# Passes of score products with up to four heads, and up to two blocks for VectorE in each

## The chip, the cores and the metric

The kernel runs on one core of a Trainium2 chip. The time is device time in microseconds of one execution; several runs give a median. TensorE (PE in the profile) does the matrix products, ScalarE (ACT) and VectorE (DVE) work on their results in PSUM, GpSimd (POOL) works on SBUF, and the queues of SyncE (SP) and ScalarE start the transfers.

## What is computed

Two attention layers read the same input of 2048 rows and 512 columns, and a gate mixes them. Layer A is softmax attention with 32 heads of 16 columns, layer B is linear attention.

```python
def _A_ref(x, wqkv, wo):
    ...
    q, k, v = qkv[0], qkv[1], qkv[2]
    scores = jnp.einsum("bhqd,bhkd->bhqk", q, k) * (Dh ** -0.5)
    p = _softmax(scores, axis=-1)
    o = jnp.einsum("bhqk,bhkd->bhqd", p, v)
    return (lambda x, *d: x.transpose(*d))(o, 0, 2, 1, 3).reshape(B, S, D) @ wo

def _B_ref(x, wqkv, wo):
    ...
    phi = lambda t: jnp.where(t > 0, t + 1, jnp.exp(t)) + 1e-6
    pq, pk = phi(q), phi(k)
    kv = jnp.einsum("bhsd,bhse->bhde", pk, v)
    z = jnp.einsum("bhsd->bhd", pk)
    num = jnp.einsum("bhqd,bhde->bhqe", pq, kv)
    den = jnp.einsum("bhqd,bhd->bhq", pq, z)[..., None] + 1e-6
    ...

g = _sigmoid((x * gate_w).sum(-1, keepdims=True))
return g * a + (1 - g) * b
```

## The kernel before

**Blocks and rounds.** A block is the score product of one head, 128 keys and 512 queries: a PSUM bank of 128 x 512. A round is four heads (every second one of a group of eight, each on its own 32 rows of the systolic array) and 512 queries. It has 16 blocks of keys for each of four heads, so 64 blocks; there are 32 rounds, 2048 blocks in all. Four products of four different heads lie on different rows of the array and can run together; the head of a block u is u % 4.

**Two ways to the exponential.** Most blocks go to ScalarE: an `ACTIVATE` with Exp (L2038) reads two or three banks at once and writes bf16 to the tile `PT` (20 slots of one block). The others are "claimed" for VectorE, which forms an approximate exponential in integers: L1558 writes 16-bit integers whose bits are read as a float16 (tile `DP`, 13 buffers of four blocks each). For four claimed blocks together two more versions are made, each shifted by a constant; these adds run on VectorE (L1599) or on POOL (L1602), whichever the planner thinks sooner. So a claimed block has three products with V, a ScalarE block one. Only the last 6 of 16 key blocks of a round can be claimed (`KB2 = 10`).

**PSUM.** Eight banks. The ring has two slots, `SLOTS = [(0, 3), (3, 3)]`: banks 0 to 2 and 3 to 5. ScalarE reads one slot while TensorE fills the other. The first two banks of a slot hold a pair; the third (bank 2 or 5, a "third" below) makes it a triple, or holds a claimed block. Bank 6 holds the sum of P V of the round. Bank 7 (`misc_banks`) serves the other work, and claimed blocks; banks 6 and 7 swap roles between rounds.

**The planner.** The program is laid down at build time by a planner written in Python, which keeps an estimate of each engine's time (`PE.t`, `AC.t`, `DV.t`, `PO.t`) and puts each instruction into the fixed order of its engine. The engines follow their order, with semaphores between them. Nothing is decided on the chip. One turn of the main loop (from L1969) makes one *pass*: the score products of two or three ScalarE blocks and perhaps a claimed one, then the exponential, and then, until the next slot is free, it fills TensorE's time with P V (`pv_step`), pieces of other work (`misc_step`) or idle products that keep TensorE's clock up (`fill`).

- P V runs in sets of four products, one for each head, on different columns of the array; `MOST` limits the sets that are laid down in a row. `PV_LAG`, `PT_URGENT` and `ROOM` steer when.
- The other work is a list of steps in chains, each with a due time in passes of three blocks: the projections Q, K and V of the next head groups and the gate (A chain), layer B (B chain), the output rows and partial sums (O chain), and some early steps. A step takes bank 7, runs in pieces of matmuls, and then queues an eviction, mostly on VectorE (`push(1, ...)`).
- VectorE's queue takes items by priority: 0 for what ends a round and for a block claimed within a pass, 1 for evictions of steps and blocks claimed otherwise, 3 for the adds. `dve_load` is the planner's estimate of the work waiting there.

Before the change a block is claimed in three ways: within a pass of a pair (`claim_in_group`, in a third, or in bank 7 when no step is due); right behind a triple (`claim_beside`, in bank 7); or between two passes with a score product by itself (`misc_step`, in bank 7, if `dve_load` is under `CLAIM_LOAD`). A pass of a triple is made when its third is free within `WAIT3` and no block can be claimed.

The core of the loop before:

```python
eb = next((b for b in (b0 + 2, 7 - (b0 + 2)) if is_free(b, soon)), None)
if eb is None and not reserved() and hold[0] is None and due_step(PE.t)[0] is None:
    eb = bank_free(PE.t + 0.02)
...
if len(us) == 2 and g > last_stage:
    extra = claim_in_group(PE.t, [j for j in range(4) if j not in [u % 4 for _, u in us]])
    if extra is not None or eb != b0 + 2:
        break
```

`L685` is the line of the helper through which nearly all matmuls are issued; the profile tells them apart by their tiles (`Qpad,KT` scores, `PT,Vaug` and `DP,Vaug` P V, `warm` idle products). L970 is the exponential of layer B's features on ScalarE.

Of the kernel before, what the change touches and what calls it, by code (L numbers as in the profile page):

```python
# [17 lines left out]
STATS = {}  # L18
# [35 lines left out]
NTRI = 4  # L54
HINT_AT = 150
KB2 = 10
# [129 lines left out]
LAT = 0.11  # L186
SET_T = 0.218
MM512 = 0.216
QK_T = 0.324
# [23 lines left out]
def bass_gated_mix__mha_block__linear_attn_block__prompt_kernel(  # L213
# [26 lines left out]
    LAST_ORDER = [(2, 0), (2, 1), (2, 2), (3, 0), (3, 1), (3, 2), (2, 3), (3, 3)]  # L240
    pairs_ = [(t8, qc) for t8 in range(NT8 - 2) for qc in range(NQC)] + LAST_ORDER
    KV0, KV1 = 1.0, 1.2
    PRE_T = 3
    PRE_GAP = 5
    OUT_GAP = 8

    with ExitStack() as es:
        _cnt = [0]
# [345 lines left out]
        def dve_load(now):  # L594
            return max(0.0, DV.t - now) + sum(o[3] * (ADD_W if len(o) > 6 else 1) for it in items for o in it.ops)
# [95 lines left out]
        def f_tr(o, i):  # L691
# [12 lines left out]
           dur=1.6)  # L704
# [67 lines left out]
        def is_free(b, now):  # L772
            return b not in bank_busy and not r_bank[b].pend and max(r_bank[b].tr + LAT, r_bank[b].tw + 0.05) <= now

        def bank_free(now):
            best = None
            for b in misc_banks:
                if b in bank_busy or r_bank[b].pend:
                    continue
                t = max(r_bank[b].tr + LAT, r_bank[b].tw + 0.05)  # L780
                if t <= now and (best is None or t < best[0]):
                    best = (t, b)
            return None if best is None else best[1]
# [394 lines left out]
        def unit_aps(r, u):  # L1178
            t8, qc, half = rounds[r]
            kb, j = u // 4, u % 4  # L1180
            kt = KT[32 * j:32 * j + 32, t8 % 2, 128 * kb:128 * (kb + 1)]
            q = Qpad[32 * j:32 * j + 32, r % NQS, :]
            return kt, q, [r_KT[t8 % 2][kb // 4], r_Q[r % NQS]]
# [3 lines left out]
        def skip(r):  # L1187
            while head[r] < NU and head[r] in taken[r]:
                head[r] += 1
# [4 lines left out]
        def next_unit():  # L1194
# [7 lines left out]
                act_round[0] += 1  # L1202
            return None

        acc_round = [0]
        acc_n = [0]
        fresh = [True]
# [115 lines left out]
        def v_ready(r, u):  # L1323
            return (rounds[r][0], u // 16) in v_done

        PT_URGENT = 11

        started = set()
        done_j = {}
# [280 lines left out]

        Q_OFF = -4
        GPR = 14.8
        B0 = 0.8
        B1 = 21
        chains = []

# [98 lines left out]
        def due_step(now):  # L1715
            load = dve_load(now)
            due = None
            for ch in chains:
                if not ch:
                    continue  # L1720
                st = ch[0]
                if (st.target > cur_g[0] and not hurry()) or not step_ready(st, now):
                    continue
                key = st.target - (A_FIRST if ch is a_chain else 3 * A_FIRST if ch is e_chain else 0)
                if due is None or key < due[2]:
                    due = (st, ch, key)
            return due, load

        def reserved():

            return acc_n[0] >= RES_FROM or (fresh[0] and acc_round[0] > 0 and r_bank[acc_bank[0]].pend)

        def behind_by():

            return max([cur_g[0] - ch[0].target for ch in chains if ch] or [0])

        def claim_beside(now, js):

            if hold[0] is not None or reserved():
                return  # L1740
            b = bank_free(now)
            if b is None:
                return
            due, load = due_step(now)
            if load >= CLAIM_LOAD or (due is not None and (load > STARVE or cur_g[0] > due[0].target + late())):
                return
            c = can_claim(now, js)
            if c is not None:
                claim(c[0], c[1], b, True)

        def claim_in_group(now, js):

            if hold[0] is None and not reserved() and due_step(now)[0] is None and bank_free(now + 0.3) is not None:
                return None
            if dve_load(now) >= (RING_LATE if behind_by() > BEHIND else RING_LOAD):
                return None
            return can_claim(now, js)

        def misc_step(now, t_late):

            if hold[0] is not None:
                if now + (SWITCH_T if pe_mode[0] == "full" else 0.0) + hold[0][2][0][2] > t_late + OVER:
                    return False
                if hold[0][2][0][3] < 0.05 and mac_until(now + 0.35) < GATE_MAC and (hold[0][0].spare or (not fresh[0] and not r_bank[acc_bank[0]].pend)):
                    return False
                cont_step()
                return True
            b = None if reserved() else bank_free(now)
            if b is None:
                if behind_by() <= THIRD or lent[0] is not None:  # L1770
                    return False
                due, load = due_step(now)
                if due is None or due[0].keeps or now + FIRST_T > t_late + OVER:
                    return False
                b3 = next((b for b in (2, 5) if is_free(b, now)), None)
                if b3 is None or not is_free(7 - b3, t_late + WAIT3):
                    return False
                STATS["thirds"] = STATS.get("thirds", 0) + 1
                due[1].popleft()
                start_step(due[0], b3)  # L1780
                return True
            due, load = due_step(now)
            c = can_claim(now, (0, 1, 2, 3)) if load < CLAIM_LOAD else None
            if due is not None and (c is None or load > STARVE or cur_g[0] > due[0].target + late() or hurry()):
                if now + FIRST_T > t_late + OVER:
                    return False
                due[1].popleft()
                start_step(due[0], b)
                return True
            if c is not None and load < LATE_CLAIM and now + QK_T < t_late:  # L1790
                claim(c[0], c[1], b, False)
                return True
            return False
# [18 lines left out]
            STATS["fills"] = STATS.get("fills", 0) + 1  # L1812
            return True

        WAIT3 = 0.2
        THIRD = 30
        HURRY = 40
        CLAIM_FREE = 2
        FORCE_N = 1
        MOST = 3  # L1820
        OVER = 0.15
        FIRST_T = 0.43
        ROOM = 0.4
        CLAIM_LOAD = 3.7
        LATE_CLAIM = 4
        STARVE = 6
        MAC_LOW = 0.45
        MAC_END = 0.45
        FILL_T = 0.2
        FILL_AHEAD = 0.9  # L1830
        END_FROM = 44
        RING_LOAD = 3.9
        RING_LATE = 4
        BEHIND = 30
        LEND = 900
        RES_FROM = 60
        MARGIN = 0.15
        PV_LAG = 13
        LATE = 8
        LAG_END = 12  # L1840
        A_FIRST = 200
        LATE_END = 0
# [1 line left out]
        def late():  # L1844
            return LATE_END if act_round[0] >= NR - 2 else -9 if e_chain else LATE

# [121 lines left out]
        last_stage = max(stage)  # L1968
        while True:  # L1969
            us = []  # L1970
            extra = None
            b0 = SLOTS[g % 2][0]
            if lent[0] is not None and is_free(lent[0], PE.t + 0.02):
                lent[0] = None
# [2 lines left out]
            if g > last_stage and lent[0] is None and hold[0] is None and (behind_by() > LEND or (e_chain and LEND_E)) and bank_free(PE.t + 0.3) is None:  # L1977
                due, _ = due_step(PE.t + 0.3)
                if due is not None and not due[0].keeps:
                    lend = due  # L1980
            eb = None
            if g > last_stage:
                soon = PE.t + WAIT3
                eb = next((b for b in (b0 + 2, 7 - (b0 + 2)) if is_free(b, soon)), None)
                if eb is None and not reserved() and hold[0] is None and due_step(PE.t)[0] is None:
                    eb = bank_free(PE.t + 0.02)
            while len(us) < SLOTS[g % 2][1]:
                if len(us) == 2 and (away or lend is not None):
                    break
                if len(us) == 2 and g > last_stage and eb is None:  # L1990
                    break
                if len(us) == 2 and g > last_stage:
                    extra = claim_in_group(PE.t, [j for j in range(4) if j not in [u % 4 for _, u in us]])
                    if extra is not None or eb != b0 + 2:
                        break
                u = next_unit()
                if u is None:
                    break
                us.append(u)
# [21 lines left out]
            for k, (r, u) in enumerate(us):  # L2021
                kt, q, rr = unit_aps(r, u)
                fns.append(f_mm(RINGB[b0 + k], kt, q))
                for res in rr:
                    if res not in rd:
                        rd.append(res)
            if extra is not None:
                kt, q, rr = unit_aps(*extra)
                fns.append(f_mm(bank_ap(eb), kt, q))
                rd += [res for res in rr if res not in rd]  # L2030
            pe_macro(fns, reads=rd, writes=[r_bank[b0 + k] for k in range(len(us))] + ([r_bank[eb]] if extra is not None else []), dur=QK_T, mac=0.053 * len(fns), mode="rows")
            if extra is not None:
                claim(extra[0], extra[1], eb, True, in_group=True)
                STATS["in_group"] = STATS.get("in_group", 0) + 1
            elif g > last_stage and len(us) == 3:
                claim_beside(PE.t, [j for j in range(4) if j not in [u % 4 for _, u in us]])
            n = 512 * len(us)
            op(AC, lambda p0=p0, b0=b0, n=n: nc.scalar.activation(  # L2038
                PT[:, 512 * p0:512 * p0 + n], ps[:, 512 * b0:512 * b0 + n], ACT.Exp, scale=LN2 / FRAC, bias=LN_KAPPA),
# [290 lines left out]
```

## Time and profile before

| | us |
|---|---|
| median of 3 runs | 685.74 (684.61 to 687.06) |
| the profiled execution | 684.7 |
| its span, from the first to the last instruction | 683.0 |
| ScalarE, two banks: 585 instructions, duration of one | 1.218 |
| ScalarE, three banks: 81 instructions, duration of one | 1.649 |
| VectorE, claimed block: 635 instructions, duration of one | 0.685 |

A row of the groups reads: line, engine, operation, output and input tiles, shapes, count, busy time of the group, mean nanoseconds of one, and then the idle time of the engine just before them with what ended it. Busy time counts overlapping instructions once, so count times mean can be more. In the timeline a row is: start, duration, engine, line, operation, tiles, shape, count, and in brackets the idle time before it. TensorE's granted clock is 1.000 over the whole span.

### The profile page before, as it was taken

How to read it: one execution, taken by the hardware profiler on the slowest of the kernel's cores; microseconds unless marked ns; L12 is line 12 of the kernel's file. 1: busy time of each engine (PE TensorE's matmuls, PEld its weight loads, DVE VectorE, ACT ScalarE, POOL GpSimd, SP SyncE). 2: the span in 40 equal slices, each digit the busy share in tenths (PEclk: the TensorE clock that was granted, in tenths of full speed). 3: DMA queues.
4: the chain of work that ended last, by engine and by line, in shares of the span. 5: the costliest groups of instructions: out<-in, count | busy, mean ns of one | idle time of the engine just before them, and what ended most of it. 6: DMA issues, size and time to landing. Idle time of an engine off the chain costs nothing.

```text
span 683.0 us, 18997 instructions
## 1 busy us (share of the span) xinstructions
PE 661.9 (97%) x8009; PEld 201.3 (29%) x8011; DVE 575.8 (84%) x961; ACT 666.8 (98%) x706; POOL 508.9 (75%) x289
## 2 busy tenths in 40 slices
PE   8999999999999999999999999999999999999997
PEld 4322222333223222222322323322332222222223
DVE  4488888889888988996789898997989998898584
ACT  5999999999999999999999999999899999999995
POOL 5097899686679797787468898776887687977770
PEclk9999999999999999999999999999999999999999
DMA  9800101000010001102001010100211201010111
GB/s 225 241 3 9 27 2 33 3 18 18 2 34 2 18 18 39 28 2 63 4 17 26 10 35 17 25 12 19 48 24 36 38 19 41 16 42 18 28 37 46
DMA packets 44815, 22.95 MB, mean 34 GB/s; under 512 B 33976, under 2 KB 40568, under 8 KB 44728
## 3 DMA queue, kind: packets, MB, share of 16 engines
q1 hardware_dynamic: 42712, 20.12, 12.9%
q10 hardware_dynamic: 2016, 1.57, 0.9%
q8 instruction: 66, 1.08, 0.6%
q14 instruction: 21, 0.17, 0.1%
HBM read 8.00 MB, written 2.10 MB: 15 GB/s over the span
## 4 chain that ended last, share of the span: by engine, by line
ACT 89%; PE 9%; DVE 1%; issue 0%; DMA 0%; SPq 0%; POOL 0%; DVEq 0%; ACTq 0%; POOLq 0%
ACT PT L2038 87%; PE ps L685 9%; ACT epool L970 2%; PE ps L692 0%; DMA rsum<-oraw 0%; DVE DP L2140 0%; DVE DP L1558 0%; DVE epool L1397 0%; DVE OT L1278 0%; DVE epool L1398 0%; DVE phi L975 0%; SPq L604 0%; DVE KT L859 0%; DVE rraw L1272 0%; DVE DP L2145 0%
## 5 line engine op out<-in xcount | busy, mean ns | idle before, releaser
L2038 ACT ACTIVATE PT<-ps 128x1024 bf16<-128x1024 f32 (+1 forms) x666 | 654.7, 1270 | 2.5 <-PE ps L685 2.3
L1602 POOL TENSOR_TENSOR DP<-DP,step 128x1024 int32<-128x1024 int32 x256 | 485.6, 1923 | 149.4 <-DVE DP L1599 50.2
L1558 DVE TENSOR_SCALAR DP<-ps 128x512 int16<-128x512 f32 x635 | 417.1, 685 | 59.3 <-PE ps L685 54.7
L685 PE MATMUL ps<-Qpad,KT 32*128 32x512 bf16 x2048 | 270.8, 384 | 13.4 <-ACT PT L2038 7.5
L685 PE MATMUL ps<-DP,Vaug 128*32 128x512 f16 x1890 | 191.0, 384 | 0.7 <-POOL DP L1602 0.2
L685 PE MATMUL ps<-PT,Vaug 128*32 128x512 bf16 x1402 | 153.5, 384 | 0.8 <-DVE Vaug L914 0.5
L685 PEld LDWEIGHTS ps<-Qpad,KT 32*128 32x128 bf16 x2048 | 67.3, 91 | 276.7 <-ACT PT L2038 250.5
L685 PEld LDWEIGHTS ps<-DP,Vaug 128*32 128x32 bf16 x1890 | 47.3, 95 | 67.0 <-issue 40.6
L685 PEld LDWEIGHTS ps<-PT,Vaug 128*32 128x32 bf16 x1402 | 36.4, 94 | 50.3 <-issue 41.3
L1599 DVE TENSOR_SCALAR DP<-DP 128x2048 int16<-128x2048 int16 (+1 forms) x62 | 45.9, 771 | 0.4 <-PE ps L685 0.4
L685 PE MATMUL ps<-warm 128*32 128x512 bf16 (+1 forms) x232 | 38.5, 390 | 1.1 <-POOL step L735 1.1
L685 PE MATMUL ps<-xT,wA 128*32 128x512 bf16 x432 | 32.3, 384 | 0.0
L1299 DVE COPY oraw<-ps 128x512 f32<-128x512 f32 x31 | 21.1, 681 | 3.3 <-PE ps L685 3.1
L970 ACT ACTIVATE epool<-ps 128x512 bf16<-128x512 f32 x32 | 23.3, 727 | 0.0
L1287 POOL TENSOR_TENSOR OT<-oraw,rbc 128x512 bf16<-128x512 f32 x12 | 15.3, 1275 | 7.6 <-DVE DP L1599 4.0
L685 PE MATMUL ps<-xT,wB 128*32 128x512 bf16 x256 | 19.1, 384 | 0.0
L685 PE MATMUL ps<-wB,xT 128*32 128x512 bf16 x256 | 18.9, 383 | 0.0
L685 PE MATMUL ps<-woA,OT 128*32 128x512 bf16 (+1 forms) x226 | 18.5, 383 | 0.0
L914 DVE CAST Vaug<-ps 128x512 bf16<-128x512 f32 x16 | 11.0, 684 | 6.5 <-PE ps L685 6.5
L975 DVE SCALAR_TENSOR_TENSOR phi<-ps,epool 128x512 bf16<-128x512 f32 x24 | 16.2, 680 | 0.0
L685 PE MATMUL ps<-wA,xT 128*128 128x128 bf16 x192 | 14.7, 220 | 0.0
L859 DVE CAST KT<-ps 128x512 bf16<-128x512 f32 (+1 forms) x16 | 10.7, 667 | 4.4 <-PE ps L685 4.4
(106 smaller groups left out, 245.8 us busy)
## 6 DMA issues: line engine op xcount, KB each, us to landing
rbc<-oraw SPq DMA_DIRECT2D x16, 256.0 KB
OT<-in_A_x_dram SPq DMA_DIRECT2D x4, 512.0 KB, 7.7
Qpad<-Qs SPq DMA_DIRECT2D x124, 16.0 KB, 1.8
oraw<-oraw SPq DMA_DIRECT2D x60, 32.0 KB, 1.9
wA<-in_A_wqkv_dram SPq DMA_DIRECT2D x1, 1536.0 KB, 8.4
wB<-in_B_wqkv_dram SPq DMA_DIRECT2D x1, 1536.0 KB, 9.0
out_dram<-outt SPq DMA_DIRECT2D x12, 128.0 KB, 1.7
phi<-in_A_x_dram ACTq DMA_DIRECT2D x3, 256.0 KB, 6.1
```

The lines of the kernel that those rows point to most:

```text
L685: return lambda: nc.tensor.matmul(o, lhsT=l, rhs=r, start=start, stop=stop, skip_group_check=sg)
L859: push(1, [(lambda: nc.vector.tensor_copy(KT[:, par, c0:c1], src), [r_bank[b]], [r_KT[par][t]], d_psum(n), None)])
L914: ops = [(lambda: nc.vector.tensor_copy(v_group(NQC * par + v)[:, :, :, 0:16], src), [r_bank[b]], [r_V[par][v]], d_psum(512), lambda: v_do ...
L970: op(AC, lambda: nc.scalar.activation(epool[:, s, :], bank_ap(b), ACT.Exp), reads=[r_bank[b]], writes=[r_e[s]], dur=0.6, issue=0.48)
L975: (lambda: nc.vector.scalar_tensor_tensor(out=dst, in0=bank_ap(b), scalar=0.0, in1=epool[:, s, :], op0=ALU.max, op1=ALU.add), [r_bank[b], ...
L1287: push(1, [(lambda: (nc.gpsimd if on_pool else nc.vector).tensor_tensor(OT[:, t8, 512 * qc:512 * (qc + 1)], oraw[:, 0, :], rbc[:], ALU.mul ...
L1299: push(0, [(lambda: nc.vector.tensor_copy(oraw[:, half, :], acc), [r_acc], [r_oraw[half]], d_psum(512), evicted)])
L1558: push(0 if in_group else 1, [(lambda: nc.vector.tensor_scalar(DP[:, i, 512 * k:512 * (k + 1)].bitcast(I16), bank_ap(b), FRAC - Y_BIAS4, Y ...
L1599: ops = (lambda z=z, i2=i2, y=y, n=n: nc.vector.tensor_single_scalar(DP[:, i2, 0:n].bitcast(I16), y, STEPS[z], ALU.add), mine_, out_, d_sb ...
L1602: ops = (ops[0], mine_ + [r_step], out_, ops[3], None, POOL_ADD, lambda z=z, i2=i2, y=DP[:, i, 0:n].bitcast(I32), n=n: nc.gpsimd.tensor_te ...
L2038: op(AC, lambda p0=p0, b0=b0, n=n: nc.scalar.activation(PT[:, 512 * p0:512 * p0 + n], ps[:, 512 * b0:512 * b0 + n], ACT.Exp, scale=LN2 / F ...
```

## The change

- `claim_beside` and `claim_in_group` go. `second_claim` is new: it looks for a second block of another head, if there is room in the `DP` buffers for it.
- A pass now lists its free extra banks (`more`): at most one third (`THIRDS = 1`; its own, else the other slot's), and bank 7, if it is free within 0.1 us and no step has the bank. A due step keeps bank 7 back only when it is over `LATE_M = 100` late.
- With two extra banks the pass takes two ScalarE blocks and two claimed ones, or, if no second claim can be had, three ScalarE blocks and one claimed. With one extra bank it takes two and one. If no block is claimed and the own third is free, it takes three. All its products are issued together.
- The claim between passes is switched off (`ALONE = 0`).
- `MOST` goes from 3 to 4 sets of P V in a row. `PV_LAG`, `PT_URGENT`, `ROOM`, `MARGIN`, `WAIT3`, the limits on VectorE's load, `CLAIM_FREE`, `LEND`, `LATE` and some due times (`B0`, `PRE_T`, `PRE_GAP`, `OUT_GAP`) change. The planner then lays down the whole order anew.

```diff
-    PRE_T = 3
-    PRE_GAP = 5
-    OUT_GAP = 8
+    PRE_T = 5
+    PRE_GAP = 6
+    OUT_GAP = 6
...
+        def peek():
+            r = act_round[0]
+            if r >= NR:
+                return None
+            skip(r)
+            return head[r] % 4 if head[r] < NU else None
...
-        PT_URGENT = 11
+        PT_URGENT = 12
...
-        B0 = 0.8
+        B0 = 0.4
...
-        def claim_in_group(now, js):
-
-            if hold[0] is None and not reserved() and due_step(now)[0] is None and bank_free(now + 0.3) is not None:
+        def second_claim(c, now, js):
+
+            r, u1 = c
+            if tri[0] is None:
+                if len(free_buffers()) < 2:
+                    return None
+            elif len(tri[0][1]) >= NTRI - 1:
                 return None
-            if dve_load(now) >= (RING_LATE if behind_by() > BEHIND else RING_LOAD):
+            elif len(tri[0][1]) == NTRI - 2 and len(closing) > MOST_OPEN:
                 return None
-            return can_claim(now, js)
+            if left(r) < 3 + MIN_LEFT:
+                return None
+            u = next((u for u in range(NU - 1, 4 * KB2 - 1, -1) if u >= head[r] and u % 4 in js and u not in taken[r] and u != u1), None)
...
-            c = can_claim(now, (0, 1, 2, 3)) if load < CLAIM_LOAD else None
+            c = can_claim(now, (0, 1, 2, 3)) if ALONE and load < CLAIM_LOAD else None
...
-        WAIT3 = 0.2
+        WAIT3 = 0.05
+        WAIT_M = 0.1
+        THIRDS = 1
+        LATE_M = 100
+        TWO_LOAD = 4
+        ALONE = 0
...
-        CLAIM_FREE = 2
+        CLAIM_FREE = 1
...
-        MOST = 3
+        MOST = 4
...
-        ROOM = 0.4
-        CLAIM_LOAD = 3.7
+        ROOM = 0.6
+        CLAIM_LOAD = 3.2
...
-        STARVE = 6
+        STARVE = 5
...
-        RING_LOAD = 3.9
+        RING_LOAD = 4
...
-        LEND = 900
+        LEND = 140
...
-        MARGIN = 0.15
-        PV_LAG = 13
-        LATE = 8
+        MARGIN = 0.19
+        PV_LAG = 14
+        LATE = 12
...
-            eb = None
+            more = []
             if g > last_stage:
                 soon = PE.t + WAIT3
-                eb = next((b for b in (b0 + 2, 7 - (b0 + 2)) if is_free(b, soon)), None)
-                if eb is None and not reserved() and hold[0] is None and due_step(PE.t)[0] is None:
-                    eb = bank_free(PE.t + 0.02)
+                more = [b for b in (b0 + 2, 7 - (b0 + 2)) if is_free(b, soon)][:THIRDS]
+                due = due_step(PE.t)[0] if hold[0] is None else None
+                if not reserved() and hold[0] is None and (due is None or cur_g[0] <= due[0].target + LATE_M):
+                    eb = bank_free(PE.t + WAIT_M)
+                    if eb is not None:
+                        more.append(eb)
...
-                if len(us) == 2 and g > last_stage and eb is None:
+                if len(us) == 2 and g > last_stage:
+                    own, j3 = b0 + 2 in more, peek()
+                    load = dve_load(PE.t)
+                    if more and load < (RING_LATE if behind_by() > BEHIND else RING_LOAD):
+                        js = [j for j in range(4) if j not in [u % 4 for _, u in us]]
+                        three = own and len(more) > 1 and load >= TWO_LOAD and j3 in js
+                        c = can_claim(PE.t, [j for j in js if not three or j != j3])
+                        c2 = None
+                        if c is not None and len(more) > 1 and not three:
+                            c2 = second_claim(c, PE.t, [j for j in js if j != c[1] % 4])
+                            three = own and c2 is None and j3 in js and j3 != c[1] % 4
+                        if c2 is not None:
+                            extras = [(c, more[0]), (c2, more[1])]
+                        elif c is not None:
+                            extras = [(c, more[1 if three else 0])]
+                    if own and b0 + 2 not in [b for _, b in extras] and j3 is not None and j3 not in [u % 4 for _, u in us + [c for c, _ in extras]]:
+                        us.append(next_unit())
                     break
...
-            if extra is not None:
-                claim(extra[0], extra[1], eb, True, in_group=True)
-                STATS["in_group"] = STATS.get("in_group", 0) + 1
-            elif g > last_stage and len(us) == 3:
-                claim_beside(PE.t, [j for j in range(4) if j not in [u % 4 for _, u in us]])
+            for c, eb in extras:
+                claim(c[0], c[1], eb, True, in_group=True)
```

More of the change, by code (lines that the diff above doesn't have):

```diff
@@ L1735, in behind_by @@
             return max([cur_g[0] - ch[0].target for ch in chains if ch] or [0])
[L1737 to L1749, printed above, removed]
-        def claim_in_group(now, js):
-            if hold[0] is None and not reserved() and due_step(now)[0] is None and bank_free(now + 0.3) is not None:
+        def second_claim(c, now, js):
[4 more added lines that the diff above has]
+            elif len(tri[0][1]) >= NTRI - 1:
                 return None
-            if dve_load(now) >= (RING_LATE if behind_by() > BEHIND else RING_LOAD):
+            elif len(tri[0][1]) == NTRI - 2 and len(closing) > MOST_OPEN:
                 return None
-            return can_claim(now, js)
+            if left(r) < 3 + MIN_LEFT:
+                return None
+            u = next((u for u in range(NU - 1, 4 * KB2 - 1, -1) if u >= head[r] and u % 4 in js and u not in taken[r] and u != u1), None)
+            if u is None:
+                return None
+            kt, q, rd = unit_aps(r, u)
+            for res in rd:
+                if res.pend or res.w is None or res.tw + LAT > now:
+                    return None
+            return r, u
         def misc_step(now, t_late):
@@ L1970, in bass_gated_mix__mha_block__linear_attn_block__prompt_kernel @@
             us = []
-            extra = None
+            extras = []
             b0 = SLOTS[g % 2][0]
@@ L1989, in bass_gated_mix__mha_block__linear_attn_block__prompt_kernel @@
                     break
-                if len(us) == 2 and g > last_stage and eb is None:
+                if len(us) == 2 and g > last_stage:
[15 more added lines that the diff above has]
+                        us.append(next_unit())
                     break
[L1992 to L1995, printed above, removed]
                 u = next_unit()
@@ L2026, in bass_gated_mix__mha_block__linear_attn_block__prompt_kernel @@
                         rd.append(res)
-            if extra is not None:
-                kt, q, rr = unit_aps(*extra)
+            for c, eb in extras:
+                kt, q, rr = unit_aps(*c)
                 fns.append(f_mm(bank_ap(eb), kt, q))
                 rd += [res for res in rr if res not in rd]
-            pe_macro(fns, reads=rd, writes=[r_bank[b0 + k] for k in range(len(us))] + ([r_bank[eb]] if extra is not None else []), dur=QK_T, mac=0.053 * len(fns), mode="rows")
-            if extra is not None:
-                claim(extra[0], extra[1], eb, True, in_group=True)
-                STATS["in_group"] = STATS.get("in_group", 0) + 1
-            elif g > last_stage and len(us) == 3:
-                claim_beside(PE.t, [j for j in range(4) if j not in [u % 4 for _, u in us]])
+            pe_macro(fns, reads=rd, writes=[r_bank[b0 + k] for k in range(len(us))] + [r_bank[eb] for _, eb in extras],
+                     dur=QK_T, mac=0.053 * len(fns), mode="rows")
+            for c, eb in extras:
+                claim(c[0], c[1], eb, True, in_group=True)
+            STATS["claims %d+%d" % (len(us), len(extras))] = STATS.get("claims %d+%d" % (len(us), len(extras)), 0) + 1
             n = 512 * len(us)
```

## The prediction

> **What bounds the kernel now.** I read the busy shares first, then the groups of instructions by shape, the chain that ended last, the waits, and the timeline of TensorE.
>
> ```profile
> span 683.0 us, 18997 instructions
> PE 661.9 (97%) x8009; PEld 201.3 (29%) x8011; DVE 575.8 (84%) x961; ACT 666.8 (98%) x706; POOL 508.9 (75%) x289
> ACT 89%; PE 9%; DVE 1%; issue 0%; DMA 0%; SPq 0%; POOL 0%; DVEq 0%; ACTq 0%; POOLq 0%
> ```
>
> ScalarE is busy for 666.8 of 683.0 us, and 89% of the chain that ended last is ScalarE. A high busy share of TensorE means less, since its matmuls overlap. So the question is what ScalarE does, and whether anybody makes it wait.
>
> ```profile
> L2038 ACT ACTIVATE PT<-ps 128x1024 bf16<-128x1024 f32 x585 | 557.4, 1218 | 1.9 <-PE ps L685 1.7
> L2038 ACT ACTIVATE PT<-ps 128x1536 bf16<-128x1536 f32 x81 | 120.1, 1649 | 0.6 <-PE ps L685 0.5
> L970 ACT ACTIVATE epool<-ps 128x512 bf16<-128x512 f32 x32 | 23.3, 727 | 0.0
> ```
>
> Nobody does: its exponentials waited 1.9 + 0.6 us in the whole run. They overlap (one takes 1.218 us from issue to end, and the next starts sooner), so their pitch is taken from the chain:
>
> ```profile
> 71.02 0.49 ACT epool L970
> 71.51 7.33 ACT PT L2038 x8
> ```
>
> A pair costs 7.33 / 8 = 0.916 us. That these eight are pairs follows from the price: a triple is longer by 1649 - 1218 = 431 ns, so eight triples would take 10.8 us. A triple costs 0.916 + 0.431 = 1.347 us. One block of 512 columns is therefore worth 0.431 us, and one instruction by itself 0.916 - 2 x 0.431 = 0.054 us. Check: 585 x 0.916 + 81 x 1.347 + 32 x 0.49 = 535.9 + 109.1 + 15.7 = 660.7 us; the remaining 22.3 us of the span are the two ends and small waits. **The time is the number of blocks left to ScalarE.** These are 585 x 2 + 81 x 3 = 1413 of 2048; VectorE took the other 635.
>
> Now the engine that would have to take more.
>
> ```profile
> L1558 DVE TENSOR_SCALAR DP<-ps 128x512 int16<-128x512 f32 x635 | 417.1, 685 | 59.3 <-PE ps L685 54.7
> L1599 DVE TENSOR_SCALAR DP<-DP 128x2048 int16<-128x2048 int16 (+1 forms) x62 | 45.9, 771 | 0.4 <-PE ps L685 0.4
> L1602 POOL TENSOR_TENSOR DP<-DP,step 128x1024 int32<-128x1024 int32 x256 | 485.6, 1923 | 149.4 <-DVE DP L1599 50.2 <-DVE DP L1558 44.3 <-DVE epool L973 20.5
> DVE DP L1558 <- PE ps L685: 54.7, 180, 2.6
> ```
>
> VectorE stood idle 59.3 us ahead of claimed blocks, 54.7 of them because the score product had not come: 180 gaps of 0.30 us. So some of VectorE's idle time is hunger for blocks, and that is what a pass with two of them can feed. POOL was idle for 149.4 us ahead of its adds.
>
> **The change part by part.** *A block more for VectorE* takes 0.431 us from ScalarE. On VectorE it costs 0.685 us and half an add (four blocks share two adds): 62 of 318 adds were VectorE's, so 0.5 x 62/318 x 0.771 = 0.075 us, together 0.76. On POOL it costs 0.5 x 256/318 x 1.923 = 0.77 us. On TensorE it has three P V products where ScalarE's block has one, so two more, half a set of four.
>
> How many more come? The ends are none and 59.3 / 0.76 = 78 blocks (34 us). A second block needs two free banks in the same pass: a third of a ring slot and bank 7. Bank 7 also serves 119 steps of other work (40 of the A chain, 58 of B, 15 of the output, 6 early ones, counted in the code), so it is often taken. Until now the blocks with a pass to themselves used that bank in order to build up stock. I counted 48 such passes in the starts of score products; they were already there while the 54.7 us of hunger stood. I stay near that row and take a quarter of the idle time, 14.8 / 0.76 = **20 blocks**: 20 x 0.431 = **8.6 us off ScalarE**. A quarter is a choice, not a measurement. VectorE pays 20 x 0.76 = 15.2 us out of those 59.3, POOL 20 x 0.77 = 15.4 out of 149.4. Without that cover nothing of it would come.
>
> *No block alone.* The first and the last of the 48, and a pass of four for comparison (columns: start, duration, group):
>
> ```profile
> 29.95 0.70 PE L685 MATMUL ps<-Qpad,KT 32*128 32x512 bf16 x4
> 30.58 0.40 PE L685 MATMUL ps<-PT,Vaug 128*32 128x512 bf16 x4
> 649.10 0.52 PE L685 MATMUL ps<-Qpad,KT 32*128 32x512 bf16 x4
> 649.54 0.39 PE L685 MATMUL ps<-DP,Vaug 128*32 128x512 f16 x2
> 289.28 0.39 PE L685 MATMUL ps<-Qpad,KT 32*128 32x512 bf16 x4
> 289.61 0.40 PE L685 MATMUL ps<-DP,Vaug 128*32 128x512 f16 x4
> ```
>
> With three products together and one behind them, P V began 0.63 and 0.44 us after the pass; with four together 0.33. That is 0.11 to 0.30 us of TensorE for each, 0.2 taken: 48 x 0.2 = 9.6 us. It costs TensorE nothing elsewhere, and ScalarE gains nothing directly, as it didn't wait for TensorE. It does pay for the P V of the added blocks: 20 x 0.5 sets x 0.217 us (the price is below) = 2.2 us.
>
> *P V in longer runs.*
>
> ```profile
> 135.80 0.39 PE L685 MATMUL ps<-Qpad,KT 32*128 32x512 bf16 x3
> 136.12 0.82 PE L685 MATMUL ps<-PT,Vaug 128*32 128x512 bf16 x10
> 136.88 0.39 PE L685 MATMUL ps<-Qpad,KT 32*128 32x512 bf16 x3
> 137.20 0.62 PE L685 MATMUL ps<-DP,Vaug 128*32 128x512 f16 x8
> 137.75 0.39 PE L685 MATMUL ps<-Qpad,KT 32*128 32x512 bf16 x3
> 345.11 0.39 PE L685 MATMUL ps<-Qpad,KT 32*128 32x512 bf16 x2
> 345.43 1.04 PE L685 MATMUL ps<-DP,Vaug 128*32 128x512 f16 x15
> 346.41 0.39 PE L685 MATMUL ps<-Qpad,KT 32*128 32x512 bf16 x3
> ```
>
> From pass to pass: two sets of four 137.75 - 136.88 = 0.87 us, three sets (ten products and two of another source) 1.08, four sets (fifteen and one) 1.30. A set is worth about 0.217. Two sets fit under a pair's 0.916, four under a triple's 1.347, and three under neither without loss or slack. So a limit of four suits triples. Behind a pair a fourth set makes the pass late by 1.30 - 0.916 = 0.38 us. The other half of the ring, on which ScalarE works meanwhile, covers that; without the cover it is 0.38 us for each such run. I cost it at nothing.
>
> *Pairs and triples.* Now 2.12 blocks ride on one instruction (1413 / 666). With 1393 blocks that is 657 instructions, 9 x 0.054 = **0.5 us less**. Bounds: all pairs, 697 instructions and +1.7 us, since the third bank is waited for by 0.05 us rather than 0.2; or 2.5 blocks each, 557 and -5.9 us. I keep the present mix.
>
> *Order laid down anew, and the waits in it.* VectorE's queue is in order: behind a claimed block or an eviction that waits stands everything else, the steps' evictions and the adds, and for these wait TensorE's passes. The trace has one case:
>
> ```profile
> 477.81 0.35 DVE L1272 RECIPROCAL rraw<-rsum 128x32 f32<-128x32 f32 x1 [2.58 <-DMA rsum<-oraw]
> 479.48 1.02 ACT L2038 ACTIVATE PT<-ps 128x1024 bf16<-128x1024 f32 x1 [1.28 <-PE ps L685]
> 480.68 3.79 ACT L2038 ACTIVATE PT<-ps 128x1024 bf16<-128x1024 f32 x4 [0.17 <-PE ps L685]
> ```
>
> VectorE stood 2.58 us for a transfer, and ScalarE lost 1.28 + 0.17 = 1.45 us. A new order has its own misses: between none more and the rival below, I take one more, **+1.5 us**. The steps issue the same transfers from SP's queue, earlier or later. The gaps of the output and of the last partial sums, and the earlier start of the B chain, move work that lies beside ScalarE; 0, within 1 us either way at the end.
>
> **Sum:** -8.6 - 0.5 + 1.5 = -7.6 us. The profiled execution took 684.7 us (span 683.0 and 1.7 around it): 677.1. The median of the runs is 685.74, 1.0 above it, so I forecast **678.1 us**.
>
> **Rivals.**
>
> *The blocks only change places.* The second blocks replace the 48 lone ones and VectorE is no fuller, because the adds get in its way:
>
> ```profile
> 308.33 1.54 DVE L1599 TENSOR_SCALAR DP<-DP 128x2048 int16<-128x2048 int16 x1 [0.36 <-PE ps L685]
> ```
>
> This add took 1.54 us, twice the group's mean of 0.771. If all of some 70 were so, 70 x (1.54 - 0.77) = 54 us of VectorE, nearly the 59.3 that are to be had. Then the time stays at 685.74 within 1.5. Against it: the mean says that few are. *The Trainium skill, "SBUF — State Buffer", section "Who interferes with whom", has the rule behind such a row: a VectorE instruction in a two-port mode and a GpSimd instruction lock each other out for their whole length. By it the change is worth less the more adds there are; the trace agrees in that row, and its mean of 0.771 says that the order mostly keeps the two apart.* Chance 0.15.
>
> *Slower: due steps come late.* The new passes take bank 7 for a block even when a step is due, until it is 100 passes late, and a block in the pass is put ahead of the steps' evictions. A projection that isn't ready when its scores are due is then forced into TensorE's queue between two passes. Its price is that of the one stall shown, 1.45 us. It decides from 9.1 / 1.45 = 7 such steps. One in ten of 119 is 12: 685.7 - 9.1 + 17.4 = 694. For it: bank 7 is the only bank of the steps. Against: between passes a due step now has the bank without competition. Chance 0.12.
>
> *More than forecast.* Half the idle time filled, 39 blocks, and 2.25 blocks on one instruction (1374 / 2.25 = 611): -16.8 - 3.0 = -19.8, 666 us. Chance 0.15; for it speaks POOL's idle time, against it bank 7.
>
> **How the numbers follow.** Forecast, 670 to 683.5: 0.58; fuller VectorE 0.15; changed places 0.15; late steps 0.12. About 0.3% (2.1 us) is what a measurement of this kernel can tell from no change. Faster 0.58 + 0.15 = 0.73, same 0.15, slower 0.12. The range of 667 to 688 leaves out about 0.08 below (most of the fuller case) and 0.1 above.
>
> **What would show it.** Right: the claimed blocks (the VectorE group from scores to DP) rise from 635 to some 655, the two exponential groups hold 1393 blocks, the idle time before claimed blocks falls from 59.3 to about 45, and ScalarE's exponentials still wait under 5 us. Changed places: the count stays within 5 of 635. Late steps: the exponentials wait over 10 us for TensorE. The pitch of pairs and triples must not move; if it does, the whole sum is wrong.

## The result, and the profile after

The changed kernel takes 675.41 us (675.2 to 675.69), the one before 685.55 in the same runs: ratio 0.985, 95% interval 0.9832 to 0.9869. It is faster by 10.1 us; 7.6 were forecast. The kernel before scatters from 684.6 to 687.1 us, and the two profiled executions (684.7 and 675.2) lie 9.5 us apart.

The profile of the changed kernel: its busy shares, its groups by shape, and one row of the chain that ended last.

```profile
span 673.4 us, 19207 instructions
PE 655.0 (97%) x8078; PEld 200.1 (30%) x8080; DVE 576.0 (86%) x968; ACT 660.0 (98%) x715; POOL 550.8 (82%) x311
```

```profile
L2063 ACT ACTIVATE PT<-ps 128x1024 bf16<-128x1024 f32 x629 | 590.9, 1130 | 0.0
L1609 POOL TENSOR_TENSOR DP<-DP,step 128x1024 int32<-128x1024 int32 x278 | 527.0, 1925 | 99.1 <-DVE DP L1565 27.6 <-DVE epool L973 21.7 <-DVE DP L1606 14.9
L1565 DVE TENSOR_SCALAR DP<-ps 128x512 int16<-128x512 f32 x654 | 433.0, 685 | 69.1 <-PE ps L685 62.9
L2063 ACT ACTIVATE PT<-ps 128x1536 bf16<-128x1536 f32 x45 | 65.1, 1517 | 0.6 <-PE ps L685 0.5
```

```profile
59.30 7.33 ACT PT L2063 x8
```

```profile
L1606 DVE TENSOR_SCALAR DP<-DP 128x2048 int16<-128x2048 int16 (+1 forms) x50 | 33.4, 696 | 0.0
```

Read them against the prediction's. A pair still costs 7.33 / 8 = 0.916 us, so the prices hold: in both traces the median distance from one end to the next is 0.917 us where a pair ends and 1.343 where a triple does. VectorE has 654 blocks instead of 635. ScalarE has 1394 left, in 629 pairs, 45 triples and one single: 675 instructions. At the forecast's prices that is 1394 x 0.431 + 675 x 0.054 = 637.3 us, where it was 645.0: **7.7 of the span's 9.6 us are on ScalarE's bill.** In the idle column the waits of the exponentials fell from 1.9 + 0.6 to 0.0 + 0.6 us, but that column is not what late starts cost, as the experiment on TensorE shows below. By the distances of the ends they cost 3.5 us before and 2.4 after. The remaining 0.9 us lie ahead of the first exponential's end (0.8) and behind the last one (0.1).

Two rows are not as forecast. VectorE's idle time ahead of claimed blocks *rose*, from 59.3 to 69.1 us, with 19 more blocks. And triples became rarer, 45 for 81, instead of keeping their share.

### The profile page after: what moved, and what is told of

The parts are those of the page before. It is cut to its first block, busy times and chain, and to the rows that moved or that the text cites. A ratio compares the mean times of both kernels' runs of the same rounds, so it can differ in the third digit from the quotient of the medians.

```text
span 673.4 us, 19207 instructions
## 1 busy us (share of the span) xinstructions
PE 655.0 (97%) x8078; PEld 200.1 (30%) x8080; DVE 576.0 (86%) x968; ACT 660.0 (98%) x715; POOL 550.8 (82%) x311
## 4 chain that ended last, share of the span: by engine, by line
ACT 95%; PE 4%; DMA 1%; DVE 1%; issue 0%; ACTq 0%
ACT PT L2063 92%; PE ps L685 3%; ACT epool L970 2%; DMA PT<-in_A_x_dram 1%; DVE DP L2165 0%; DVE xT L1909 0%; PE ps L692 0%; DVE KT L859 0%; DVE DP L2170 0%; DVE flag L2175 0%; ACT eg L954 0%; ACTq L2278 0%
## 5 line engine op out<-in xcount | busy, mean ns | idle before, releaser
L2063 ACT ACTIVATE PT<-ps 128x1024 bf16<-128x1024 f32 (+1 forms) x675 | 648.1, 1155 | 0.7 <-PE ps L685 0.5
L1609 POOL TENSOR_TENSOR DP<-DP,step 128x1024 int32<-128x1024 int32 x278 | 527.0, 1925 | 99.1 <-DVE DP L1565 27.6
L1565 DVE TENSOR_SCALAR DP<-ps 128x512 int16<-128x512 f32 x654 | 433.0, 685 | 69.1 <-PE ps L685 62.9
L685 PE MATMUL ps<-Qpad,KT 32*128 32x512 bf16 x2048 | 264.6, 384 | 10.0 <-ACT PT L2063 4.7
L685 PE MATMUL ps<-DP,Vaug 128*32 128x512 f16 x1949 | 206.8, 384 | 1.6 <-DVE oraw L1306 0.7
L685 PE MATMUL ps<-PT,Vaug 128*32 128x512 bf16 x1384 | 174.3, 384 | 0.6 <-DVE Vaug L914 0.5
L685 PEld LDWEIGHTS ps<-PT,Vaug 128*32 128x32 bf16 x1384 | 42.1, 95 | 46.7 <-issue 36.7
L685 PE MATMUL ps<-warm 128*32 128x512 bf16 (+1 forms) x272 | 46.7, 387 | 1.1 <-POOL step L735 1.1
L1606 DVE TENSOR_SCALAR DP<-DP 128x2048 int16<-128x2048 int16 (+1 forms) x50 | 33.4, 696 | 0.0
L970 ACT ACTIVATE epool<-ps 128x512 bf16<-128x512 f32 x32 | 23.4, 731 | 0.0
L975 DVE SCALAR_TENSOR_TENSOR phi<-ps,epool 128x512 bf16<-128x512 f32 x24 | 16.3, 681 | 0.0
L685 PEld LDWEIGHTS ps<-warm 128*32 128x32 bf16 (+1 forms) x272 | 11.6, 98 | 13.8 <-issue 12.1
```

The lines of the kernel that those rows point to most:

```text
L685: return lambda: nc.tensor.matmul(o, lhsT=l, rhs=r, start=start, stop=stop, skip_group_check=sg)
L970: op(AC, lambda: nc.scalar.activation(epool[:, s, :], bank_ap(b), ACT.Exp), reads=[r_bank[b]], writes=[r_e[s]], dur=0.6, issue=0.48)
L975: (lambda: nc.vector.scalar_tensor_tensor(out=dst, in0=bank_ap(b), scalar=0.0, in1=epool[:, s, :], op0=ALU.max, op1=ALU.add), [r_bank[b], ...
L1565: push(0 if in_group else 1, [(lambda: nc.vector.tensor_scalar(DP[:, i, 512 * k:512 * (k + 1)].bitcast(I16), bank_ap(b), FRAC - Y_BIAS4, Y ...
L1606: ops = (lambda z=z, i2=i2, y=y, n=n: nc.vector.tensor_single_scalar(DP[:, i2, 0:n].bitcast(I16), y, STEPS[z], ALU.add), mine_, out_, d_sb ...
L1609: ops = (ops[0], mine_ + [r_step], out_, ops[3], None, POOL_ADD, lambda z=z, i2=i2, y=DP[:, i, 0:n].bitcast(I32), n=n: nc.gpsimd.tensor_te ...
```

## The experiments

The theory to test: the time is ScalarE's bill, 0.431 us for each block it keeps and 0.054 for each instruction. Rivals: TensorE is just as tight, and the passes saved there are the gain; VectorE is full; the gain is the luck of a new order, not the new passes.

### Twenty microseconds on each engine in turn

The order of the changed kernel stays as it is, and one engine gets work that the planner doesn't know of.

ScalarE, in every 16th pass:

```diff
+            if g % 16 == 8:
+                op(AC, lambda b0=b0: nc.scalar.activation(scr[:], ps[:, 512 * b0:512 * b0 + 512], ACT.Exp, scale=LN2 / FRAC, bias=LN_KAPPA),
+                   reads=[r_bank[b0]], writes=[r_scr], dur=0.0, issue=0.0)
```

> The changed kernel with its order untouched; 42 exponentials are preceded by one more of 512 columns into a scratch tile (the planner is told it takes no time). One is worth 0.431 + 0.054 = 0.485 us of ScalarE. My theory (ScalarE's bill sets the time): 42 x 0.485 = 20.4 us, so 675.4 + 20.4 = 695.8 us, within 2. Rival (TensorE or VectorE bounds the kernel as much as ScalarE, and the ScalarE row only looks full because its instructions overlap): well under that, 675 to 685 us.

VectorE, ahead of every 22nd claimed block:

```diff
+            if n_claim[0] % 22 == 11:
+                items[-1].ops.appendleft((lambda: nc.vector.tensor_scalar(scr[:], bank_ap(b), FRAC - Y_BIAS4, Y_BIAS4, op0=ALU.max, op1=ALU.add),
+                                          [r_bank[b]], [r_scr], 0.0, None))
```

> The changed kernel with its order untouched; before 30 of the 654 claimed blocks VectorE reads the bank once more into a scratch tile, 30 x 0.685 = 20.6 us of VectorE that the planner doesn't know of. My theory (VectorE is hungry, and the time is ScalarE's): under 4 us more, 675.4 to 679.4, as the 69.1 us of idle time ahead of claimed blocks take it up. Rival (VectorE is full wherever it matters): up to 20.6 us more, 696 us.

TensorE, with every fifth run of P V:

```diff
+            if n_run[0] % 5 == 2 and len(started) == 4:
+                fns += [f_mm(acc[32 * j:32 * j + 32, :], warm[:, 0:32], warm4, start=False, stop=False, sg=True) for j in range(4)]
```

> The changed kernel with its order untouched; 100 runs of P V get one set of four idle products more (of zeros, added to the sum), 100 x 0.217 = 21.7 us of TensorE that the planner doesn't know of. My theory: some of these passes come late, but the other half of the ring covers most; under 8 us more, 675.4 to 683. Rival (TensorE is the second bound, and the passes to themselves were saved there): about 21.7 us more, 697 us.

| added to | us added | time | more than 675.41 | share paid |
|---|---|---|---|---|
| ScalarE | 20.4 | 694.18 | 18.8 | 92% |
| TensorE | 21.7 | 687.19 | 11.8 | 54% |
| VectorE | 20.6 | 681.35 | 5.9 | 29% |

The microseconds added are estimates from prices of the traces: 0.485 for each of 42 exponentials, 0.685 for each of 30 readings of a bank, 0.217 for each of 100 sets of four products. ScalarE is the bound: 42 extra exponentials cost 18.8 / 42 = 0.447 us each. For the other two the expectations missed: under 4 us for VectorE and under 8 for TensorE. They pay only a part, but each delays some of the passes. The groups of the kernel with more on TensorE show how such a delay looks:

```profile
L685 PE MATMUL ps<-warm 128*32 128x512 bf16 x588 | 58.7, 379 | 0.0
L2069 ACT ACTIVATE PT<-ps 128x1024 bf16<-128x1024 f32 x629 | 594.3, 1059 | 3.4 <-PE ps L685 1.1
L2069 ACT ACTIVATE PT<-ps 128x1536 bf16<-128x1536 f32 x45 | 64.0, 1477 | 1.0 <-PE ps L685 0.7
```

There are 588 idle products of this shape instead of 188, and the span is 685.4 us, 12.0 longer than that of the changed kernel. Yet the exponentials' idle time rose only from 0.6 to 4.4 us. The rest is not in that column.

In an unbroken row of pairs ScalarE's recorded starts lie 0.904 us apart and the ends 0.917, so each pair lasts some 12 ns longer than the one before it: in the kernel before, from 1.184 to 1.272 us over the eight pairs that start between 71.2 and 77.6 us. A start that is late by less than has gathered in this way costs nothing. In the changed kernel the start at 322.71 us is 0.075 us late, the instruction takes 1.033 us after one of 1.096, and the ends stay 0.916 apart. A later one moves the ends and can still leave no gap: the start at 303.41 us is 0.096 us late and the ends lie 0.994 apart, though the pair ahead ends only at 303.44.

So a late start is priced from the ends: by how much they lie further apart than the undisturbed 0.917 us (a triple 1.343, one bank 0.490); distances within 0.02 us are left out. Summed over the traces:

| kernel | late ends | us lost by them |
|---|---|---|
| changed | 36 | 2.4 |
| with more on VectorE | 75 | 8.4 |
| with more on TensorE | 124 | 14.1 |
| with more on ScalarE | 11 | 0.8 |

The 6.0 and 11.7 us more are, within 0.1 us, all that was paid for VectorE and for TensorE. With more on ScalarE it is the other way round: its queue is longer, more late starts are covered, and 42 x 0.490 - 1.6 = 19.0 us are near the 18.8 paid. The mean duration is no such measure. It falls with late starts, whether that costs time or not (1059 ns here, 1130 in the changed kernel, 1218 in the one before), and the kernel before has the longest mean and loses more than the changed one. So **the idle column understates ScalarE's waiting, and the distance between the ends shows it**.

### The change in parts

Constants alone: the old passes with the new values (16 constants, `MOST = 4` among them).

```diff
-        WAIT3 = 0.2
+        WAIT3 = 0.05
...
-        MOST = 3
+        MOST = 4
```

> The kernel before, with all constants of the changed kernel that it has (PRE_T to LATE, MOST = 4 among them), planned anew; passes as before. The order laid down has 631 blocks for VectorE, 1417 for ScalarE in 682 exponentials: 1417 x 0.431 + 682 x 0.054 = 647.6 us, against 645.0 before. My theory (the bill): 685.6 + 2.6 = 688.2 us, within 2.5. Rival (the constants, longer runs of P V above all, bring the gain by relieving TensorE): 676 to 681 us.

Passes alone: the changed kernel with the old values.

```diff
-        WAIT3 = 0.05
+        WAIT3 = 0.2
...
-        MOST = 4
+        MOST = 3
```

> The changed kernel with all constants as before, planned anew: passes of up to four, two blocks for VectorE, no block alone. The order has 630 blocks for VectorE, 1418 for ScalarE in 667 exponentials: 1418 x 0.431 + 667 x 0.054 = 647.2 us against 645.0 before. My theory (the bill): 685.6 + 2.2 = 687.8 us, within 2.5, slower than before although no block has a pass to itself. Rival (the passes bring the gain, by TensorE's saved time): 676 to 681 us.

No second block:

```diff
         def second_claim(c, now, js):
 
+            return None
```

> The changed kernel with no second block for VectorE in a pass, planned anew. The order has 613 blocks for VectorE, 1435 for ScalarE in 670 exponentials: 1435 x 0.431 + 670 x 0.054 = 654.7 us against 637.3. My theory: 675.4 + 17.4 = 692.8 us, within 3. Rival (second blocks only change places with blocks that would be claimed in the next pass): within 3 of 675.4.

Blocks alone again:

```diff
-        ALONE = 0
+        ALONE = 1
```

> The changed kernel with blocks alone allowed again (ALONE = 1), planned anew. The order has 628 blocks for VectorE, 1420 for ScalarE in 673 exponentials: 1420 x 0.431 + 673 x 0.054 = 648.4 us against 637.3. My theory (a block alone takes bank 7 from the passes, so fewer are claimed): 675.4 + 11.1 = 686.5 us, within 3. Rival (a block alone costs only its TensorE time, 0.2 us each, which is covered): within 3 of 675.4.

Runs of three:

```diff
-        MOST = 4
+        MOST = 3
```

> The changed kernel with MOST = 3, planned anew. The order laid down leaves 2048 - 648 = 1400 blocks to ScalarE in 670 exponentials: 1400 x 0.431 + 670 x 0.054 = 639.6 us, against 1394 x 0.431 + 675 x 0.054 = 637.3 in the changed kernel. My theory (the bill): 675.4 + 2.3 = 677.7 us, within 1.5. Rival (the longer runs by themselves save TensorE switches and so time): 680 us or more.

Each plans its order anew, so a block more or less comes from the whole order and not from the edited line alone. The bill is worked out from the groups of each profile; all differences are to the changed kernel. "Late" is what late ends cost, as above; "ends" are the stretch up to the first exponential's end and the one behind the last.

| kernel | blocks left to ScalarE | its exponentials | bill | late | ends | span | time | time, difference |
|---|---|---|---|---|---|---|---|---|
| changed | 1394 | 675 | 0 | 0 | 0 | 0 | 675.41 | 0 |
| runs of three | 1400 | 670 | +2.3 | -0.2 | +0.8 | +2.9 | 677.95 | +2.5 |
| before | 1413 | 666 | +7.7 | +1.0 | +0.9 | +9.6 | 685.55 | +10.1 |
| passes alone | 1418 | 667 | +9.9 | +2.6 | +3.9 | +16.3 | 690.20 | +14.8 |
| constants alone | 1417 | 682 | +10.3 | +2.7 | +2.4 | +15.4 | 690.54 | +15.1 |
| blocks alone again | 1420 | 673 | +11.1 | +2.0 | +3.8 | +16.9 | 691.87 | +16.5 |
| no second block | 1435 | 670 | +17.4 | -0.1 | +0.4 | +17.5 | 692.70 | +17.3 |

The bill puts the parts nearly in their order. It comes within 0.2 us of the time's difference for runs of three and for no second block. For passes alone, constants alone and blocks alone again it is short by 4.8 to 5.4 us, so the last of these missed its expectation (686.5 within 3); the first two, forecast from the kernel before, lie at the edge of theirs (2.4 and 2.3 us off, within 2.5). The three terms divide the span, so they must add up to it (here within 0.2 us). What they show is where the rest lies: partly at the ends and partly in late starts. Rows of ScalarE for it; first blocks alone again, then constants alone:

```profile
L2063 ACT ACTIVATE PT<-ps 128x1024 bf16<-128x1024 f32 x597 | 565.2, 1147 | 1.9 <-PE ps L685 1.7
ACT DP L2159 <- PE ps L685: 6.9, 1, 6.9
```

```profile
L2038 ACT ACTIVATE PT<-ps 128x1024 bf16<-128x1024 f32 x629 | 593.0, 1163 | 2.6 <-PE ps L685 2.6
ACT DP L2134 <- PE ps L685: 6.3, 1, 6.3
```

and the changed kernel:

```profile
ACT DP L2159 <- PE ps L685: 3.8, 1, 3.8
```

The last kind of row is ScalarE waiting, after its last exponential, for the first row block of the output: 6.9 and 6.3 us instead of 3.8. So 3.1 and 2.5 us are a longer end.

**Neither half of the change is faster by itself.** The new passes at the old constants have no block alone, so their TensorE time is saved, and the kernel is slower than before (ratio 1.0062, interval 1.0043 to 1.0082); the new constants on the old passes too (1.0068, 1.0049 to 1.0087). With that, the rival falls by which TensorE's saved time alone is the gain.

How the blocks for VectorE are spread over the passes, in the order that the planner lays down:

| kernel | passes | with one such block | with two | blocks by themselves | blocks in all |
|---|---|---|---|---|---|
| before | 666 | 568 | 0 | 67 | 635 |
| changed | 675 | 562 | 46 | 0 | 654 |
| no second block | 670 | 613 | 0 | 0 | 613 |
| passes alone | 667 | 514 | 58 | 0 | 630 |
| blocks alone again | 673 | 522 | 28 | 50 | 628 |

So the second blocks first of all replace the blocks by themselves (67 in that order, where the prediction counted 48 in the trace), and without them 41 of the 654 are missing. But they don't make the count by themselves: passes alone has more passes with two, 58, and only 630 blocks, because 95 of its passes carry none, against 67 in the changed kernel. There the constants come in. Blocks alone again agrees with its theory: 50 go by themselves, and only 550 passes carry any, against 608. Without second blocks VectorE is hungrier than in any other run:

```profile
L1565 DVE TENSOR_SCALAR DP<-ps 128x512 int16<-128x512 f32 x613 | 415.3, 687 | 100.2 <-PE ps L685 95.5
```

### Steps that come late

The kernel before with one constant changed:

```diff
-        LATE = 8
+        LATE = 12
```

> The kernel before with LATE = 12 alone, planned anew: the other work may wait longer before it goes ahead of a claim. The order has 635 blocks for VectorE as before, 1413 for ScalarE in 665 exponentials, so the bill is 644.9 us against 645.0. By the bill alone 685.5 us, within 2. By the rival of the prediction (steps that come late hold up scores): several waits of about 1.45 us each, 692 us or more.

695.71 us, ratio 1.0139 (1.0114 to 1.0164), with the same number of blocks. The bill's 685.5 within 2 missed. The rival's size was about right and its place wrong. The groups and waits of ScalarE:

```profile
L2038 ACT ACTIVATE PT<-ps 128x1024 bf16<-128x1024 f32 x582 | 554.4, 1230 | 0.3 <-PE ps L685 0.2
ACT DP L2134 <- PE ps L685: 17.9, 1, 17.9
```

No score is held up: the pairs wait 0.3 us, and only 13 ends are late. The loss is all at the end, where the wait is 17.9 us and the kernel before has 4.0; by late ends this kernel loses 2.1 us less. TensorE's timeline there shows what was late:

```profile
676.13 1.05 PE L685 MATMUL ps<-woB,OBT 128*32 128x512 bf16 x16 [0.86 <-DVE outt L1163]
677.01 1.04 PE L685 MATMUL ps<-woA,OT 128*32 128x512 bf16 x16
678.99 1.05 PE L685 MATMUL ps<-woB,OBT 128*32 128x512 bf16 x16 [0.95 <-DVE outt L1163]
```

These are output rows that are otherwise worked off beside the exponentials. Now they come one after the other, and each row block (a product with woB and one with woA) waits until VectorE has emptied the bank.

### Luck of the order

Old passes with constants drawn at random; the order that the planner liked best of 100:

```diff
-        WAIT3 = 0.2
+        WAIT3 = 0
...
-        MARGIN = 0.15
+        MARGIN = 0.21
```

> The kernel before with its old kinds of pass, blocks alone among them, and constants drawn at random, the best of 100 draws by the planner (PT_URGENT 12, B0 1.0, WAIT3 0, CLAIM_FREE 1, MOST 4, ROOM 0.6, RING_LOAD 4.4, MARGIN 0.21, LATE 4). The order has 641 blocks for VectorE, 1407 for ScalarE in 684 exponentials: 1407 x 0.431 + 684 x 0.054 = 643.4 us against 645.0 before. By the bill: 685.6 - 1.6 = 684.0 us, within 2.5. If the gain of the change were the luck of a new order and not the new passes, the old passes would reach 678 or less as well.

New passes, the best of as many draws:

```diff
-        ROOM = 0.6
+        ROOM = 0.7
...
-        PV_LAG = 14
+        PV_LAG = 15
```

> The changed kernel with its new passes and constants drawn at random as for the old passes, the best of as many (100) draws by the planner. The order has 657 blocks for VectorE, 1391 for ScalarE in 673 exponentials: 1391 x 0.431 + 673 x 0.054 = 635.9 us against 643.4 for the old passes with the best of 100. If the new passes are worth something at the same luck: 680.6 - 7.5 = 673.1 us, within 3. If the gain is the luck of the order: 679 us or more, as the old passes.

Old passes 680.56 us (ratio 0.9914, 0.989 to 0.9938), new ones 676.96 (0.9864, 0.9837 to 0.9891). Both missed their expectation, by about 1 us beyond its bounds, on opposite sides. So a new order alone brought the old passes 5 of the 10.1 us (1.6 by the bill, 1.2 by late ends, 1.2 at the two ends of the span, the rest scatter of the kernel before), and at equal luck the new passes are ahead by 680.56 - 676.96 = 3.6 us. The bill put them 7.5 us ahead; but their order loses 2.7 us more by late ends (4.9 against 2.2) and 1.1 more at the end. One pair of draws is no proof of that share; each kernel's interval is narrow, but another draw would give another order.

### More of it

The changed kernel with seven constants moved:

```diff
-        POOL_ADD = 1.97
+        POOL_ADD = 1.9
...
-        THIRDS = 1
+        THIRDS = 2
...
-        MOST = 4
+        MOST = 5
...
-        MARGIN = 0.19
+        MARGIN = 0.17
```

> The changed kernel with seven constants moved (POOL_ADD 1.97 to 1.9, nearer to the 1.925 us that the profile shows for POOL's add; THIRDS 1 to 2, MOST 4 to 5, MARGIN 0.19 to 0.17, PT_URGENT 12 to 13, Q_OFF -4 to -6, YIELD_SOON 0.5 to 0.3), planned anew. The order has 662 blocks for VectorE, 1386 for ScalarE in 669 exponentials: 1386 x 0.431 + 669 x 0.054 = 633.5 us against 637.3. By the bill: 675.4 - 3.8 = 671.6 us, within 2.5. Rival (VectorE and TensorE have so little room left that eight more blocks come back as waits): 675 us or more.

674.91 us (674.14 to 675.65), ratio 0.9832 (0.981 to 0.9854): not to be told from the changed kernel. The blocks came and the time did not:

```profile
L2063 ACT ACTIVATE PT<-ps 128x1024 bf16<-128x1024 f32 x619 | 583.1, 1114 | 1.1 <-PE ps L685 0.7
L1565 DVE TENSOR_SCALAR DP<-ps 128x512 int16<-128x512 f32 x662 | 435.4, 684 | 62.6 <-PE ps L685 57.9
```

The bill fell by 3.8 us and the time by 0.5; the expectation of 671.6 within 2.5 missed, and 674.91 is 0.1 us short of the rival's 675. It went the rival's way: late ends cost 5.6 us instead of 2.4, at 63 exponentials instead of 36, of which the idle column shows 1.2.

## Why the prediction was right, and where it was not

- **ScalarE's bill.** Right. Over nine other orders it missed the difference by 0.1 to 5.4 us, and by 12.7 only where the end was upset (late steps); work added to ScalarE cost 92% of itself. What the bill misses lies in late starts and at the ends. *The Trainium skill, "Perfetto Trace Analysis", section "Optimizing Scalar/DVE Operations", gives about 51 ns of access overhead for a ScalarE instruction on PSUM; the 0.054 us of the trace agree.* The medians from start to start, 0.478 us for one bank (L970), 0.904 for two and 1.331 for three, leave 0.051 beside 0.427 a block; from end to end it is 0.064.
- **Twenty blocks.** 19 came, 19 x 0.431 = 8.2 us. The number was a choice, and that it was met is luck: the working behind it failed. A quarter of VectorE's idle time was to be used, leaving 45 us; it rose to 69.1. VectorE's busy time hardly moved (575.8 and 576.0). The claimed blocks took 433.0 - 417.1 = 15.9 us more, and the adds 45.9 - 33.4 = 12.5 us less, because POOL took 278 of the adds instead of 256 and the mean add on VectorE fell from 0.771 to 0.696 us. POOL paid with 41.4 us, and its idle time fell from 149.4 to 99.1. So the step that failed is the cover: not the hunger ahead of claimed blocks, but POOL's idle time. Why the hunger stays with blocks to be had was not tried by itself; bank 7, which I named as the limit, is unproven.
- **Instructions.** Wrong in sign: 9 more, not 9 fewer, +0.5 us for -0.5. The bound with fewer triples was the right side; that a third now more often carries a claimed block where it made a triple is read from the code and wasn't tried.
- **New waits.** Wrong in sign: late ends cost 1.0 us less (3.5 and 2.4; in the idle column 2.5 and 0.6), where one stall more was forecast (+1.5). Together: -8.2 + 0.5 for the bill, -1.0 for late ends and -0.9 at the two ends are the span's -9.6.
- **No block alone, longer runs.** Nothing directly, as forecast: runs of three cost 2.5 us, and the bill has 2.3 of it. But "nothing" held only because the new order fits; TensorE pays 54% of what is put on it blindly, more than the cover I had named.
- **Rivals.** Blocks that change places: in part. The second blocks do replace those by themselves, but 19 more came on top; the passes alone end at such a count (630). The lock between VectorE and POOL, which that rival rested on, became no rarer; it turned. The low mean didn't say that the order keeps the two apart, as I had read it. An add on VectorE and a POOL instruction meet 28 times in the trace before and 27 times after, and whichever starts second is stretched. That was VectorE's add 7 times before (1.09 to 2.33 us instead of 0.69) and twice after (0.77 and 1.75); otherwise it was POOL's instruction (its add then takes 2.27 us instead of 1.89). Hence VectorE's lower mean. Late steps: they did not come with this change; in the run where they came (`LATE` = 12), they lengthened the end and held up no score.

What stays open is how much of the 10.1 us is due to the kind of pass and how much to the fit between passes and constants. Each half alone is slower than before; together they are faster. The counts say how the halves need each other, not why these constants let more passes carry a block.

## What to carry to other kernels

Write the bill of the engine that bounds, price by price, from the distance between ends and not from durations, and judge an edit by what it takes off that bill. In a kernel whose order a planner lays down, the constant `LATE` by itself moved the time by 10 us, so compare two designs each with its own tuned constants, and count the blocks before thinking about mechanisms. When the bill doesn't explain a loss, look at the end of the trace first, and then for late ends.

## What the runs showed that I had not expected

ScalarE's busy share says nothing of its slack: it was 98% before and after, and still 98% with 20.6 us more on VectorE and 97% with 21.7 us more on TensorE. Its instructions overlap, so a late start first shortens the recorded duration of the instruction (between 1.02 and 1.37 us for the same pair), then moves its end, and only then opens a gap.
